# Lightning attention and a four-expert mixture on one core: unit 4's second product nested as well, attention's steps drawn together, preparation lists joined

## The chip, the core and the metric

The kernel runs on one core of a Trainium2 chip, in fp32 throughout. The metric is the device time of one execution in microseconds. The core has a matrix engine (TensorE, PE in the profile, with its weight loads as PEld), three engines for elementwise work (VectorE or DVE, ScalarE or ACT, GpSimd or POOL), and SyncE (SP), which here does nothing but issue DMA transfers. The engines run side by side, each through its own list of instructions in program order, and wait for each other by semaphores.

## The reference, cut to what matters

```python
# attention: q, k, v of (4 batches, 8 heads, 768 tokens, 64), blocks of 64 tokens, a decay lam per head
for b in range(12):
    intra = (qb @ kb^T * Dmask) @ vb                      # per batch and head
    inter = (qb * lam_pow) @ kv_state
    out[block b] = intra + inter
    kv_state = lam**64 * kv_state + (kb * rev_pow)^T @ vb
x = out of all heads side by side                         # (3072, 512)
p = domain_probs / (sum of domain_probs + 1e-9)           # (3072, 4)
for e in range(4):
    h = relu(x @ w1[e])                                   # 512 -> 1024
    y += p[:, e:e+1] * (h @ w2[e])                        # 1024 -> 512
```

The state `kv_state` goes from block to block of one batch and head, so attention has an order in time; the mixture has none, but each of its tokens needs its attention output first.

## The kernel before, in words

**Units.** The 3072 tokens are cut into three groups of 1024, each of eight chunks of 128 tokens. A unit is a group with an expert: twelve units, in the order that `ORDER` gives (group 0 with experts 0 to 3, group 1 with 1, 2, 3, 0, group 2 with 2, 3, 0, 1). A unit has a first product (x @ w1) and a second (h @ w2). Both are computed by Strassen-Winograd: seven products M1 to M7 of half-size blocks instead of eight, with sums of blocks before and after. The first product is *nested*: each of its seven products is again cut into seven, which makes 98 matmuls of 128x256 in a unit. It is `first_product`, whose matmul is line 1195. The second product exists in two forms: `second_product` (line 1254) goes one level deep, with 112 matmuls in a unit; `nested_product` (line 1571) goes two levels, with 98. `NEST` (line 140) is the first unit whose second product is nested. It is `2 * E - 3`, which is 5.

**Iterations and slots.** One iteration `at` of the main loop at the end of the kernel interweaves the second product of unit `at` with the first product of unit `at + 1`. It has seven parts `i`, one for each M, and each of those eight steps `x`. `(at * 7 + i) * 8 + x` counts the steps; I call the number a slot. The text's "unit 2" as a stretch of time is the iteration `at` = 2, slots 112 to 167.

**Attention.** Chunks 0 to 7 (group 0) are done in the prologue. Chunks 8 to 23 are spread over the iterations: `AT` (line 906) gives each its slot. At that slot the step `both` puts the values of the chunk before (`values`, matmuls at lines 842 and 860, over the state `kv` and over the masked scores) and the scores and new state of this one (`scores`, lines 779 and 786) into TensorE's order, 64x64 matmuls between the large ones. Ahead of that, counted back from the slot, come the loads (`load` of v 7 slots ahead unless `V_AHEAD` says otherwise, of k by `K_AHEAD`), the regrouping of k on ACT (`regroup`, line 526), the decay of k on POOL (`decayed`), and turning q and k on DVE (`turn`). After a pair of chunks, `pair_sums` makes sums of the x blocks on POOL (tile `to`) and stores them to `x_blocks`, from which `x_fill` loads the operands `xs` of a later group, and `x_inner` adds up more of them on POOL.

**Preparing weights.** Nested products need sums of weight blocks. They do not depend on x, and POOL makes them once for each expert, in lists of steps: load raw blocks (`w1b`, `w2b`), make totals of 512 columns (`w1o`, `w2o`), then, for each M, four sums of 256 columns (`ops`, in `inner` and `inner_w2`), and store them to DRAM (`w1_ops`, `w2_ops`, `w2_sums`). `prepare_w1`, `prepare_w2` and `prepare_w2_ops` give such lists; their steps stand in `chores`. Before, the lists follow each other whole, and that of `prepare_w2_ops(1)` is appended when `at` reaches `NEST`. The operands come back with loads named `ws_in<-w1_ops`, `w2t<-w2_sums` and `w2t<-w2_ops`.

**What sets the order.** Nothing is scheduled at run time; the Python program writes each engine's order. `pump` (line 208) is called once in every slot and takes a step from `chores` when a small model of the clock allows it: `now` counts slots, `busy` is until when POOL is estimated to be occupied (`tt`, line 116: columns / 480 slots, / 640 from unit `NEST` on, where `spare` holds), `moved` and `asked` the same for DMA. Behind a step, `pump` keeps a distance: 4 or 7 slots if `spare`, else 1. Stores are held back in `queue` by `store` until `busy` says that POOL is done. SP issues all of these loads and stores in the order of the program, each when its operands are there. `until(what)` forces steps out of `chores` until something is made, and `feed`, `feed2`, `feed3` issue the loads of products to come. DVE work that is not urgent stands in `background`, `lately`, `aside` and `own_sums`.

**The gates.** The factors p lie in `gate` (for 16 chunks) for units that are not nested. For nested units they are broadcast over the tile `decay`, which attention uses too: the load into `gate_bc` is issued at `NEST - 1`, `i` = 2, so attention has to be over by then. `turn_gates` stores the factors by rows.

**The change of form.** Group 1 begins with plain units (4 is the last of them in this kernel) and ends with nested ones. The plain unit's output rows are parked in DRAM as `partial` in the last step of unit `NEST - 1` (line 1273); in `first_result`, `gather` loads them as `po` and `finish_rows` adds them on POOL to the nested units' sums, which lie across and are turned.

Of the kernel before, what the change touches and what calls it, by code (L numbers as in the profile page):

```python
# [21 lines left out]
def kernel(  # L22
# [93 lines left out]
    def tt(eng, o, a, b, op):  # L116
        eng.tensor_tensor(out=o, in0=a, in1=b, op=op)  # L117
        if eng is nc.gpsimd:
            busy[0] = max(busy[0], now[0]) + math.prod(o.shape[1:]) / (640 if spare else 480)
        else:  # L120
            vector(math.prod(o.shape[1:]), PSUM in (a.space, b.space))
# [18 lines left out]
    NEST = 2 * E - 3  # L140
# [55 lines left out]
    LEFT, packed, resting = 1, [], [False]  # L196
    FULL = 4
# [10 lines left out]
    def pump(pace=1.0, force=False):  # L208
# [11 lines left out]
        if begins:  # L220
# [3 lines left out]
            free[0] = max(free[0], begin + max(pace * (busy[0] - was), (4 if len(chores) > 13 else 7) if spare else 1))  # L224
# [11 lines left out]
    def inner(eng, what, to, blk, ops, at):  # L236

        b = {n: blk[:, i, j * 256:(j + 1) * 256] for n, (i, j) in at.items()}
        s = stage.tile([P, 4, 256], FP32, name="ops", tag="st")
        for i, (name, x, y, op) in enumerate(ops):  # L240
            b[name] = s[:, SLOT[name]]
            tt(eng, b[name], b[x], b[y], op)
        pieces = [(to[:, 1:5], s[:])]
        if A_OF[what[2]][0] == "S":
            pieces += [(to[:, 0], blk[:, 0, 0:256]), (to[:, 5:7], blk[:, 1].rearrange("p (a f) -> p a f", a=2))]
# [12 lines left out]
    def inner_w1(e, m, blk):  # L258
        at = {"A11": (0, 0), "A21": (0, 1), "A12": (1, 0), "A22": (1, 1)}
        inner(nc.gpsimd, ("w1", e, m), w1_ops[e, MS.index(m)], blk, S_OPS, at)  # L260
# [13 lines left out]
    def prepare_w1(e):  # L274
        st = {}

        def block(name, i, j):
            t = stage.tile([P, 2, W], FP32, name="w1b", tag="st")
            src = moe_w1[e, j * 256:(j + 1) * 256, i * W:(i + 1) * W]
            send(out=t[:], in_=src.rearrange("(c p) f -> p c f", p=P))  # L280
            st[name] = t

        def total(name, a, b, op):
            t = stage.tile([P, 2, W], FP32, name="w1o", tag="st")
            halves(t[:], st[a][:], st[b][:], op)
            st[name] = t

        def ready(m):
            inner_w1(e, m, st[A_OF[m]])

        return weight_steps(block, total, ready)
# [64 lines left out]
    def prepare_w2_ops(e, eased):  # L356
# [39 lines left out]
        def drop(*names):  # L396
# [3 lines left out]
        return [  # L400
            lambda: (block("A21", 1, 0), block("A22", 1, 1)), pause(6),
            lambda: total("S1", "A21", "A22", ALU.add),
            lambda: (ready("M4"), block("A11", 0, 0), drop("A22")), pause(4),
            less, lambda: ready("M7"), lambda: (ready("M1"), drop("S3")), lambda: ready("M5"),
            lambda: (total("S2", "S1", "A11", ALU.subtract), block("A12", 0, 1)), lambda: ready("M6"),
            *([lambda: ready("M2")] if e != units[FINAL][1] else []),
            lambda: total("S4", "A12", "S2", ALU.subtract), lambda: ready("M3"),
        ]
# [21 lines left out]
    def x_fill(g, m):  # L430
# [8 lines left out]
        if g == LAST:  # L439
            own_x_apart(m, g, 8)  # L440
        else:
            chores.insert(0, lambda: x_inner(g, m))
# [175 lines left out]
    gate = consts.tile([P, LAST * CPG, E], FP32, name="gate")  # L618
# [5 lines left out]
    def gates():  # L624
# [11 lines left out]
            out=gate[:, 0:CPG].rearrange("p (h x) e -> p h x e", h=2), in_=of[:, :, 0:2].rearrange("p b c e -> p c b e"),  # L636
        )
        for g in range(1, NG):
            for h in range(2):
                n = g * CPG + h * 4  # L640
                for to in ([gate[:, n:n + 4]] if g < LAST else []) + [last[:, n - CPG:n - CPG + 4]]:
                    nc.scalar.copy(
                        out=to.rearrange("p (b c) e -> p b c e", c=2), in_=of[:, h::2, 2 * g:2 * g + 2],
                    )
# [261 lines left out]
    AT = (34, 40, 48, 54, 60, 91, 100, 108, 115, 147, 154, 167, 172, 203, 210, 223)  # L906
    K_AHEAD = {10: 14, 11: 14, 12: 15, 14: 17, 15: 18, 16: 18, 18: 17, 20: 19, 22: 17}
# [1114 lines left out]
```

## Time and profile before

| | |
|---|---|
| time, median of 3 runs | 1139.07 us (1138.53 to 1140.1) |
| profiled execution | 1138.78 us, of which the span is 1137.0 |
| PE busy | 1128.0 us (99%) |
| PEld, DVE, ACT, POOL busy | 986.1, 774.1, 445.0, 764.8 us |
| DMA | 261.36 MB, mean 230 GB/s |
| prologue, to the start of unit 0 | about 90 us |
| units 1 to 4 | 99.7, 97.6, 99.8, 94.1 us |
| units 5 and 6 | 84.6, 85.0 us |

The span runs from the first instruction to the last; about 1.8 us of the time lie around it. A unit's start is the first matmul of its iteration. In a row of the profile, L1195 is line 1195 of the kernel, then come engine, operation, tiles (out<-in) and shape; a matmul in fp32 leaves two records, so that "x8" is four matmuls of the program. L117 is the helper `tt`, through which all elementwise sums go, so those are told apart by their tiles. Row names leave the digits out: `w_ops` is `w1_ops` or `w2_ops`. In windows the columns after the length are the busy times of PE, PEld, DVE, ACT and POOL with their number of instructions, the granted clock, the DMA share and GB/s.

### The profile page before, as it was taken

What the parts mean: (1) busy time and instruction counts of PE and PEld (TensorE: products, weight loads), DVE (VectorE), ACT (ScalarE), POOL (GpSimd) and SP (SyncE); (2) the same over time, 40 slices, a digit from 0 to 9 for tenths busy, and PEclk for the clock granted to TensorE, in tenths of its full rate; (3) what the DMA queues carried; (4) which work ended last, traced back from release to release, by engine and by line L of the source; (5) the groups of instructions that cost most, each with busy time, mean ns of one, the idle gap of its engine ahead of it and who ended that gap; (6) DMA issues with size and microseconds to landing.
All of it is one profiled execution on the core that took longest, in us unless ns stands there. A gap on an engine that the chain in (4) does not pass through costs nothing.

```text
span 1137.0 us, 22208 instructions
## 1 busy us (share of the span) xinstructions
PE 1128.0 (99%) x7967; PEld 986.1 (87%) x7967; DVE 774.1 (68%) x1478; ACT 445.0 (39%) x988; POOL 764.8 (67%) x730
## 2 busy tenths in 40 slices
PE   8999999999999999999999999999999999999998
PEld 7788888888888888888888888888888888888887
DVE  4576777587587658837655566778767576776785
ACT  4325245255234534422453443344354452342332
POOL 2745547656753976644884998795984873873885
PEclk9999999999999999999999999999999999999999
DMA  9796887889896987876767669876778657656652
GB/s 200 171 281 193 227 223 233 284 273 321 259 361 209 310 270 245 286 270 216 257 195 251 189 197 319 271 225 200 224 231 253 179 161 213 188 159 205 176 195 74
DMA packets 297901, 261.36 MB, mean 230 GB/s; under 512 B 129408, under 2 KB 241216, under 8 KB 297792
## 3 DMA queue, kind: packets, MB, share of 16 engines
q1 hardware_dynamic: 287728, 255.71, 73.0%
q10 hardware_dynamic: 10032, 4.23, 1.5%
q8 instruction: 64, 1.05, 0.4%
q14 instruction: 45, 0.37, 0.1%
q0 software_dynamic: 32, 0.00, 0.0%
HBM read 192.20 MB, written 71.34 MB: 232 GB/s over the span
## 4 chain that ended last, share of the span: by engine, by line
PE 98%; DVE 1%; issue 0%; DMA 0%; ACT 0%; DVEq 0%; POOLq 0%; ACTq 0%
PE pg L1195 41%; PE pq L1571 25%; PE q L1254 21%; PE pM L1713 3%; PE pc L1713 2%; PE op L842 1%; PE sp L779 1%; PE op L860 1%; PE sp L786 1%; PE pM L1438 1%; PE pg L1571 1%; PE qp L745 0%; DMA decay<-in_lam_dram 0%; PE kp L745 0%; DVE m L117 0%
## 5 line engine op out<-in xcount | busy, mean ns | idle before, releaser
L1195 PE MATMUL pg<-xs,ws_in 128*128 128x256 f32 x1960 | 470.1, 380 | 0.1
L1195 PEld LDWEIGHTS pg<-xs,ws_in 128*128 128x128 f32 x1960 | 371.1, 190 | 52.5 <-DVE m L117 2.1
L117 DVE TENSOR_TENSOR m<-pg,m 128x512 f32<-128x512 f32 x374 | 255.3, 685 | 96.9 <-PE pg L1195 87.5
L1254 PE MATMUL q<-w2t,m 128*128 128x256 f32 x1120 | 265.4, 380 | 0.0
L1254 PEld LDWEIGHTS q<-w2t,m 128*128 128x128 f32 x1120 | 212.1, 190 | 29.6 <-issue 0.6
L117 DVE TENSOR_TENSOR sums<-pq,sums 128x256 f32<-128x256 f32 x272 | 112.9, 420 | 90.6 <-PE pq L1571 75.2
L117 POOL TENSOR_TENSOR m<-m,decay 128x512 f32<-128x512 f32 x91 | 114.5, 1271 | 85.9 <-ACT m L1212 64.6
L1571 PE MATMUL pq<-acc,w2t 128*128 128x256 f32 x688 | 169.2, 379 | 0.0
L1571 PEld LDWEIGHTS pq<-acc,w2t 128*128 128x128 f32 x688 | 130.6, 190 | 17.9
L1212 ACT ACTIVATE m<-m 128x512 f32<-128x512 f32 x99 | 62.3, 630 | 154.4 <-DVE m L117 152.3
L117 DVE TENSOR_TENSOR m<-m,m 128x512 f32<-128x512 f32 x108 | 96.9, 898 | 7.8 <-ACT m L1178 7.0
L1208 ACT COPY m<-pg 128x512 f32<-128x512 f32 x88 | 51.5, 586 | 123.4 <-PE pg L1195 115.8
L1272 DVE SCALAR_TENSOR_TENSOR acc<-q,gate,acc 128x256 f32<-128x256 f32 x108 | 52.0, 481 | 69.9 <-PE q L1254 68.9
L1172 ACT COPY pg<-m 128x512 f32<-128x512 f32 x77 | 45.4, 590 | 103.0 <-DVE m L117 88.2
L117 POOL TENSOR_TENSOR acc<-hT,hT 128x512 f32<-128x512 f32 x56 | 70.4, 1271 | 22.6 <-PE pq L1571 13.2
L117 POOL TENSOR_TENSOR acc<-hT,acc 128x512 f32<-128x512 f32 x56 | 71.2, 1272 | 6.5 <-PE pq L1571 2.9
L526 ACT COPY kx<-kn 32x128 f32<-32x128 f32 x224 | 66.2, 295 | 12.8 <-PE op L860 5.1
L1571 PE MATMUL pq<-hT,w2t 128*128 128x256 f32 x288 | 70.0, 379 | 0.0
L117 POOL TENSOR_TENSOR w2o<-w2b 128x512 f32<-128x512 f32 x26 | 35.6, 1391 | 49.2 <-DMA w2b<-in_moe_w_dram 38.2
L1571 PEld LDWEIGHTS pq<-hT,w2t 128*128 128x128 f32 x288 | 54.7, 190 | 7.4
L1176 ACT COPY m<-pg 128x512 f32<-128x512 f32 x44 | 25.7, 585 | 77.0 <-PE pg L1195 70.7
L1571 PE MATMUL pq<-m,w2t 128*128 128x256 f32 x228 | 55.4, 379 | 0.0
(158 smaller groups left out, 1465.2 us busy)
## 6 DMA issues: line engine op xcount, KB each, us to landing
ws_in<-w_ops SPq DMA_DIRECT2D x40, 512.0 KB, 4.8
w2t<-w_ops SPq DMA_DIRECT2D x72, 256.0 KB, 3.1
ws_in<-w_ops SPq DMA_DIRECT2D x60, 256.0 KB, 3.6
ws_in<-w_ops SPq DMA_DIRECT2D x40, 384.0 KB, 3.8
w2b<-in_moe_w_dram SPq DMA_DIRECT2D x56, 256.0 KB, 5.5
w_ops<-ops SPq DMA_DIRECT2D x28, 512.0 KB, 4.7
w_ops<-ops SPq DMA_DIRECT2D x54, 256.0 KB, 3.8
w2t<-w_ops SPq DMA_DIRECT2D x100, 128.0 KB, 2.7
```

The costliest lines, as they stand in the source:

```text
L117: eng.tensor_tensor(out=o, in0=a, in1=b, op=op)
L526: nc.scalar.copy(out=to[j * 32:(j + 1) * 32, :, x], in_=of[x * 32:(x + 1) * 32, :, j // 2, j % 2 * 32:(j % 2 + 1) * 32],)
L779: nc.tensor.matmul(out=sp[r][half[x], ac * BL:(ac + 1) * BL], lhsT=hc(kT)[half[r], ac, blk[x]], rhs=hc(qT)[half[r], ac, blk[x]], start=(ac ...
L1172: nc.scalar.copy(out=banks[tags[1]][:], in_=new["11"][:])
L1176: nc.scalar.copy(out=o[:], in_=p[:])
L1195: nc.tensor.matmul(out=p[:, j * 256:(j + 1) * 256], lhsT=ws[i][:, j * P:(j + 1) * P], rhs=xs[i], start=(fresh and j == 0), stop=True, skip ...
L1208: nc.scalar.copy(out=new[at][:], in_=p[:])
L1212: nc.scalar.activation(out=new[at][:], in_=new[at][:], func=AF.Relu)
L1254: nc.tensor.matmul(out=p[:, s * DH:(s + 1) * DH], lhsT=h[A_OF[m]][:, c * 256 + s * P:c * 256 + (s + 1) * P], rhs=fed2[g, e, m][uu][:, c], ...
L1272: nc.vector.scalar_tensor_tensor(out=o, in0=x, scalar=w, in1=o, op0=ALU.mult, op1=ALU.add)
L1571: nc.tensor.matmul(out=p[:, 0:256], lhsT=fed3[e, m, i][:, c * P:(c + 1) * P], rhs=b[B_OF[i]][:, c * 256:(c + 1) * 256], start=(fresh and c ...
L1713: nc.tensor.matmul(out=p[:, s * 256:(s + 1) * 256], lhsT=a[c][:, f:f + P], rhs=b[:, c, j * 256:(j + 1) * 256], start=(s == 0 and c == 0 an ...
```

## The change

- `NEST` becomes `2 * E - 4`: unit 4, the first of group 1, has its second product nested too. Group 1 is now nested as a whole, so `partial`, its stores, loads and additions go, and `gate` keeps group 0 alone.
- Attention's slots are drawn together: the last chunk's scores are at slot 172 (iteration 3) instead of 223. Chunks named in `ALONE` (12, 13, 17, 18 and the last) get a slot of their own for their values, so these no longer stand beside the next chunk's scores; scores at certain slots go to the PSUM banks s0 and s1. `V_AHEAD` goes, `K_AHEAD` is shorter.
- The lists of preparation are joined by `in_turn`: the first step of a list, its raw loads, is put ahead of the last two steps of the list before. `prepare_w2_ops(1)` is now the fourth list, from the start. M2's sums are made in all eased lists.
- The model's POOL cost becomes 0.13 + n/770 slots (0.2 + n/820 with `spare`) for n columns, and `pump` keeps 3 slots with `spare` behind a step that used POOL, else 1.
- `prepare_w1` and `inner` get an `eased` form, which is not called; the condition on `SEQ.index(m)` in `x_fill` always holds.

```diff
-    NEST = 2 * E - 3
+    NEST = 2 * E - 4
...
-            busy[0] = max(busy[0], now[0]) + math.prod(o.shape[1:]) / (640 if spare else 480)
+            n = math.prod(o.shape[1:])
+            busy[0] = max(busy[0], now[0]) + (0.2 + n / 820 if spare else 0.13 + n / 770)
...
-            free[0] = max(free[0], begin + max(pace * (busy[0] - was), (4 if len(chores) > 13 else 7) if spare else 1))
+            free[0] = max(free[0], begin + max(pace * (busy[0] - was), 3 if spare and busy[0] > was else 1))
...
+    def in_turn(*lists):
+
+        work = []
+        for of in lists:
+            n = OVER if work else 0
+            work[len(work) - n:] = [of[0], *work[len(work) - n:], *([] if n else of[1:2]), *of[2:]]
+        return work
...
-            *([lambda: ready("M2")] if e != units[FINAL][1] else []),
...
-    gate = consts.tile([P, LAST * CPG, E], FP32, name="gate")
+    gate = consts.tile([P, CPG, E], FP32, name="gate")
...
-    AT = (34, 40, 48, 54, 60, 91, 100, 108, 115, 147, 154, 167, 172, 203, 210, 223)
-    K_AHEAD = {10: 14, 11: 14, 12: 15, 14: 17, 15: 18, 16: 18, 18: 17, 20: 19, 22: 17}
-    V_AHEAD = {CPG + 10: 8, CPG + 13: 10}
+    AT = (34, 40, 48, 54, 60, 72, 91, 100, 108, 115, 130, 146, 153, 160, 167, 172)
+    ALONE = {CPG + 4: 66, CPG + 5: 79, CPG + 9: 124, CPG + 10: 137, NG * CPG - 1: 178}
+    LEAD = {}
+    K_AHEAD = {10: 14, 11: 14, 12: 15}
...
-            def both(n=n):
-                if n > first:
+            def both(n=n, s=s):
+                if n > first and n - 1 not in ALONE:
                     values(n - 1, ("s0", "s1"))
-                scores(n, ("q02", "q12"))
+                scores(n, ("s0", "s1") if 8 <= s % 56 < 32 else ("q02", "q12"))
...
-            steps.append((s - V_AHEAD.get(n, 7), lambda n=n: load(n, "v")))
+            steps.append((s - 7, lambda n=n: load(n, "v")))
...
+            if n in ALONE:
+                steps.append((ALONE[n], lambda n=n: values(n, ("s0", "s1"))))
-        steps.append((AT[last - first] + 5, lambda: values(last, ("s0", "s1"))))
-        steps.append((AT[last - first] - 14, turn_gates))
+        steps.append((ALONE[last] + 2, turn_gates))
...
-        while unit_of[g, e] in (1, 2 * E) and to_do.get(m):
+        while unit_of[g, e] in (1, E, 2 * E) and to_do.get(m):
...
-            if unit_of[g, e] in (E - 1, NEST - 1) and m in ("M2", "M6", "M5", "M3"):
-                to = rows[n] if g == 0 else partial[n % CPG * P:(n % CPG + 1) * P]
-                results.append(lambda: send(out=to[:, j * DH:(j + 1) * DH], in_=o))
+            if unit_of[g, e] == E - 1 and m in ("M2", "M6", "M5", "M3"):
+                results.append(lambda: send(out=rows[n][:, j * DH:(j + 1) * DH], in_=o))
...
-            tt(nc.gpsimd, t[:], t[:], po[:], ALU.add)
-            store(lambda: send(out=rows[CPG + n], in_=t[:]))
+            t = gathered_out.pop(n)
+            send(out=rows[CPG + n], in_=t[:])
...
-            chores.extend(prepare_w2(2) + prepare_w1(3) + prepare_w2(3))
-            chores.extend(prepare_w2_ops(2, False) + prepare_w1(0))
-            for x in (3, 0):
-                chores.extend(prepare_w2_ops(x, True))
+            chores.extend(in_turn(
+                prepare_w2(2), prepare_w1(3), prepare_w2(3), prepare_w2_ops(1, False), prepare_w2_ops(2, False),
+                prepare_w1(0), prepare_w2_ops(3, True), prepare_w2_ops(0, True),
+            ))
...
-            until(("w1", 0, "M4"))
-            chores.extend(prepare_w2_ops(1, True))
+            until(("w2", 1, "M4"))
             spare.append(True)
```

## The prediction

> **What bounds the kernel.** I read the page's busy shares first, then the chain that ended last, the windows cut at the units, and last TensorE's records around one chunk of attention.
>
> ```profile
> span 1137.0 us, 22208 instructions
> PE 1128.0 (99%) x7967; PEld 986.1 (87%) x7967; DVE 774.1 (68%) x1478; ACT 445.0 (39%) x988; POOL 764.8 (67%) x730
> PE 98%; DVE 1%; issue 0%; DMA 0%; ACT 0%; DVEq 0%; POOLq 0%; ACTq 0%
> ```
>
> TensorE is busy for 99% of the span and carries 98% of the chain, so the time is the matmuls that the program holds plus the few waits that it gets. Taking work off another engine is worth nothing here. The windows are those of units 1 to 6 and, last, 20 us inside unit 2:
>
> ```profile
> 187.80:287.50 99.70, 99.70 (x933) 87.19 (x932) 73.27 (x142) 42.36 (x115) 63.94 (x69) 1.00 0.87 284
> 287.50:385.10 97.60, 97.60 (x789) 85.11 (x788) 69.57 (x127) 41.69 (x111) 60.60 (x65) 1.00 0.91 294
> 385.10:484.90 99.80, 99.80 (x902) 87.22 (x901) 68.78 (x126) 37.81 (x101) 71.26 (x82) 1.00 0.85 269
> 484.90:579.00 94.10, 94.10 (x598) 82.83 (x598) 56.37 (x97) 29.80 (x58) 56.59 (x61) 1.00 0.74 244
> 579.00:663.60 84.60, 84.60 (x393) 74.34 (x392) 47.27 (x83) 38.70 (x80) 68.11 (x63) 1.00 0.65 205
> 663.60:748.60 85.00, 84.94 (x393) 74.31 (x393) 62.39 (x124) 32.39 (x59) 74.40 (x71) 1.00 0.84 270
> 325.00:345.00 20.00, 20.00 (x94) 17.34 (x93) 18.16 (x26) 10.18 (x29) 12.28 (x9) 1.00 1.06 377
> ```
>
> After the length come the busy times of PE, PEld, DVE, ACT and POOL, the clock, the DMA share and GB/s. TensorE never idles in units 1 to 5; a nested unit without attention (5) takes 84.6 us. Where unit 2 is densest, DVE is busy 18.2 us of 20 and DMA moves 377 GB/s, and TensorE still does not wait.
>
> ```profile
> 446.60 1.89 PE L1195 MATMUL pg<-xs,ws_in 128*128 128x256 f32 x8
> 448.42 0.69 PE L842 MATMUL op<-qx,kv 64*64 64x64 f32 x32
> 448.94 0.65 PE L860 MATMUL op<-st,vn 64*64 64x64 f32 x32
> 449.40 0.65 PE L779 MATMUL sp<-qx,kx 64*64 64x64 f32 x32
> 449.87 0.65 PE L786 MATMUL sp<-vn,kn 64*64 64x64 f32 x32
> 450.44 1.99 PE L1254 MATMUL q<-w2t,m 128*128 128x256 f32 x8
> 452.28 0.59 PE L1195 MATMUL pg<-xs,ws_in 128*128 128x256 f32 x2
> ```
>
> One chunk's values and the next one's scores stand together: a stretch of 64x64 matmuls between the large ones.
>
> **The change, part by part.** *Matmuls.* Counted in the two programs, L1254 goes from 560 to 448 large matmuls and L1571 from 602 to 700: 112 out, 98 in. Eight records (four matmuls of 128x256) follow each other in 1.727 us, 0.432 us for one. 14 fewer: -14 x 0.432 = **-6.05 us**, all on the path. It is also the difference between a plain unit (210 x 0.432 = 90.7) and the 84.6 of unit 5.
>
> *More stretches.* The 64x64 matmuls stay the same in number, but chunks with a step of their own split their stretch: counted from chunk 8 on, 17 stretches become 21. From 446.60 to 452.28 are 5.68 us: two large batches of 1.727 (3.45), four small ones of 0.466 (1.87), and 0.36 us for going in and out. 4 x 0.36 = **+1.44 us**. The stretch around 496 us (two small batches) leaves the same 0.36.
>
> *Work that moves.* Attention's last chunk goes from slot 223 to 167-178, so units 1 and 2 take six chunks or so where they had four. By their matmuls unit 1 becomes 90.7 + 20 x 0.466 + 7 x 0.36 = 102.6 us, unit 2 with 19 small batches 102.1.
>
> POOL in unit 2, counted by kind and multiplied by the page's rows: the 256-column list operations on `ops` go from 28 to 48 (21.6 to 36.0 us), the 512-column totals on `w2o` and `w1o` from 14 to 18 (19.3 to 24.5), and two more chunks bring two `kn` at 1.1, two `kv` at 0.78 and four `to` at 0.81 (7.1). In all 64.7 to 91.3 us of 102.1. Unit 1 goes from 66.6 to 74.6, unit 3 from 66.4 to 81.6, unit 4 from 55.8 to 75.8, unit 5 from 70.0 to 81.1 of 84.7. Units 3 to 5 I cost at nothing: unit 6 now does 74.4 us on POOL in 85.0 with TensorE busy 84.94, and a list that is late in unit 5 can run on in unit 6, which falls from 78.3 to 60.9.
>
> SP in unit 2: the `w2_ops` stores go from 6 to 36, those of `w1_ops` from 8 to 0, the `w2b` loads from 14 to 10, those of a chunk (`kn`, `qx`, `vn`) from 12 to 17; +3.8 MB. In unit 1 the `w2b` loads go from 8 to 22, stores and chunk loads grow by 7; +5.5 MB. SP issues in order, so every store stands with the loads behind it until POOL has done its operands: in unit 1 to 2 that was 12.3 us over 8 waits, longest 5.9. Unit 1 needs 28.3 + 5.5 = 33.8 MB in 102.6 us, 330 GB/s; unit 2 28.7 + 3.8 = 32.5 MB, 318 GB/s. At their present GB/s for a share (284/0.87, 294/0.91) that is a share of 1.01 and 0.99.
>
> [...]
>
> What this can cost, from both sides. Nothing, if all stays covered as between 325 and 345 us; less than nothing only by TensorE's own waits, 5.6 us in all, of which I grant 1.1. At the upper end POOL's chain in unit 2 is the bound:
>
> ```profile
> POOL xs L117 <- DMA xs<-x_blocks: 12.7, 1, 12.7
> POOL w2o L117 <- DMA w2b<-in_moe_w_dram: 10.9, 2, 8.4
> POOL kn L117 <- ACT kx L526: 7.4, 1, 7.4
> POOL to L117 <- DVE xc L117: 3.2, 1, 3.2
> ```
>
> These are POOL's waits in unit 2. The `w2b` one should go, since each list's first raw loads are now issued two steps before the last list ends. If the other 23.3 us stay, 91.3 + 23.3 = 114.6 us must fit in 102.1: 12.5 us late. Set beside the start of the matmul that reads it, the k decay on POOL now ends at least 6.0 us early, so TensorE would stand 6.5 us, or all 12.5 if that slack is used up as well. I take **+1.5 us**: the 20 us with everything full and no wait are the nearest row, and above it I allow a wait as long as the longest that a chunk now has on ACT's `kv` (1.0), and half of another.
>
> *At nothing.* Gone are 16 `partial` stores, 8 loads and 8 POOL additions of 1.272 us: all in nested units whose TensorE does not idle; they also take 3.1 MB off DMA there. DVE gains 49 `sums` at 0.420 and loses 24 `m<-m,m` at 0.898 and 28 `acc` at 0.481; unit 2's DVE rises from 76.3 to 83.6 of 102.1, below the 91% that the 20 us show covered. ACT's 46 to 60 us there are far from a bound. The planner's POOL cost (n/480 to 0.13 + n/770) and the pump's spacing only move the list steps that are counted above.
>
> *Sum.* The profiled execution took 1138.78 us (span 1137.0 and 1.8 around it), 0.29 below the median. 1138.78 - 6.05 + 1.44 + 1.5 = 1135.67; with the 0.29, **1136.0 us**.
>
> **The rivals.** *Loads late (the gain is eaten).* Set beside its first matmul, the tightest `ws_in` load of `w1_ops` now lands 2.9 us ahead, in unit 1. If one store in each of units 1 and 2 holds SP for the 5.9 us seen there, the loads behind it are 3.0 us late each: 6 us instead of 1.5, so 1134.5 + 6 = 1140.5; with one of them 1137.5. For it: DMA shares near 1.0, and six times as many stores of `w2_ops` behind POOL. Against it: the median slack of these loads is 13.5 us, and raw loads move ahead. I take 1139.
>
> *POOL becomes the bound of unit 2 (the other side).* The longer chain of list operations in front of the chunks' decays makes TensorE stand in the last chunks of unit 2, where three of them follow at every seventh slot (146, 153, 160). 6.5 to 12.5 us give 1141.0 to 1147.0; middle 1144. It decides from 4.6 us of waits on: there the gain is gone; from 6.9 on the loss can be measured. For it: 91.3 of 102.1 us, in an engine that takes its work in program order. Against it: the planner spaces the list steps, and the wait for `xs` is in part room that POOL had to spare, as its work ran ahead.
>
> *The change does not nest unit 4.* The order has the 98 matmuls, so this has no chance.
>
> **How the numbers follow.** The forecast has a chance of 0.45, late loads 0.20, POOL's bound 0.35. 0.2% (2.3 us) is about what a measurement can tell from no change: faster is below 1136.8, slower above 1141.35. So faster 0.45, same 0.20, slower 0.35. The range runs from 1134.5 - 1.1 = 1133.4 to the end of the third case, 1147.0; the forecast alone holds 1133.4 to 1136.8.
>
> **What the profile after would show.** The chain still at 98% PE; unit 4 near 85.0 us and units 1 and 2 at 102.6 and 102.1 if nothing waits; 21 stretches. Any excess in units 1 to 3 is the error: by POOL's bound it stands as idle of L779/L786 or L842 behind POOL `kn` or `qx` in unit 2, with POOL above 90%; by late loads as idle of L1195 behind `ws_in`. I am wrong on the other parts if units 5 to 11 change by more than 0.3 us each, or if a stretch costs other than 0.36.

## The result, and the profile after

The changed kernel takes 1165.45 us (median of 6 runs, 1161.67 to 1167.11) against 1139.64 us before: a ratio of 1.0222, 95% interval 1.0207 to 1.0237. It is 2.2% slower; I had forecast 1136.0 us. Its profiled execution, at 1161.67 us, is the fastest of the six. What follows compares its span of 1159.5 us with the 1137.0 us of before.

The page of the changed kernel: span, busy times, the chain by engine.

```profile
span 1159.5 us, 22257 instructions
PE 1130.7 (98%) x7939; PEld 982.2 (85%) x7939; DVE 786.0 (68%) x1502; ACT 453.4 (39%) x1003; POOL 817.3 (70%) x767
PE 65%; POOL 2%; DMA 2%; DVE 1%; ACT 0%; issue 0%; SPq 0%; POOLq 0%; DVEq 0%; ACTq 0%
```

TensorE has 28 records (14 matmuls) fewer and is busy for longer; its part of the chain falls from 98% to 65%. The shares add up to 70%, since the chain could be followed back only to about 332 us; even on that part POOL, DMA and DVE hold 5 of 70. Something other than TensorE sets the time in places. To see where, I cut both traces at the first first-product matmul of iterations 1, 2, 3 and 4. First before, then after; columns as earlier (length, then busy PE, PEld, DVE, ACT, POOL, clock, DMA share, GB/s).

```profile
189.50:289.30 99.80, 99.80 (x934) 87.25 (x933) 73.06 (x141) 42.35 (x115) 64.78 (x68) 1.00 0.86 282
289.30:389.00 99.70, 99.70 (x902) 87.14 (x901) 70.25 (x124) 42.46 (x115) 62.62 (x68) 1.00 0.92 298
389.00:488.70 99.70, 99.70 (x902) 87.17 (x901) 68.25 (x124) 37.78 (x100) 71.08 (x81) 1.00 0.85 266
```

```profile
189.60:305.60 116.00, 104.00 (x1061) 88.86 (x1059) 83.27 (x157) 47.14 (x133) 87.33 (x89) 0.99 0.89 297
305.60:421.10 115.50, 109.44 (x1140) 94.05 (x1141) 72.38 (x139) 53.31 (x155) 83.41 (x91) 0.96 0.91 284
421.10:517.50 96.40, 95.13 (x598) 82.41 (x598) 61.61 (x105) 29.91 (x59) 86.99 (x96) 1.00 0.85 283
```

Units 1 and 2 are longer by 16.4 and 15.8 us (99.7 to 116.1 and to 115.5), unit 3 is shorter by 3.4, unit 4 by 7.2 (91.9 to 84.7). Unit 0 is longer by 0.9 and unit 6 by 1.0; all other units agree within 0.1 us. POOL is busy for only 75% and 72% of units 1 and 2, DMA stands at 0.89 and 0.91: neither is full, and TensorE waits all the same. These are TensorE's waits in the changed kernel between 187 and 420 us (what waited and for whom; total, times, longest), below them those of POOL between 187 and 450 us from 1.4 us up, and last POOL's waits for stores in the kernel before, in the same stretch.

```profile
PE pg L1234 <- DMA ws_in<-in_moe_w_dram: 8.1, 2, 5.8
PE sp L823 <- POOL kn L117: 6.4, 2, 5.5
PE pg L1234 <- DVE m L117: 1.8, 2, 1.0
PE sp L823 <- issue: 1.8, 2, 1.3
```

```profile
POOL w2o L117 <- DMA x_blocks<-to: 17.7, 1, 17.7
POOL ops L117 <- DMA w_ops<-ops: 9.3, 1, 9.3
POOL w2o L117 <- DMA w2b<-in_moe_w_dram: 8.0, 2, 5.1
POOL xs L117 <- DMA xs<-x_blocks: 7.7, 2, 4.6
POOL w2o L117 <- DMA w_ops<-ops: 7.6, 1, 7.6
POOL w2o L117 <- DMA w_sums<-w2o: 5.5, 1, 5.5
POOL kn L117 <- ACT kx L563: 1.5, 1, 1.5
POOL to L117 <- DMA w_sums<-w2o: 1.4, 1, 1.4
```

```profile
POOL w1o L117 <- DMA x_blocks<-to: 2.5, 1, 2.5
POOL ops L117 <- DMA w_ops<-ops: 1.0, 1, 1.0
POOL w2o L117 <- DMA w_ops<-ops: 0.5, 1, 0.5
```

The rows that matter name a *store* as what POOL waits for: `x_blocks<-to`, `w_ops<-ops`, `w_sums<-w2o`. `w2o` and `ops` are not computed from those transfers. They are tiles of the same staging ring (`stage`, seven buffers for raw blocks, totals, sums and `to`), and a new tile may be written only when the one that had its buffer has been stored. 17.7 + 9.3 + 7.6 + 5.5 + 1.4 = 41.5 us go this way. In the kernel before it was 4.0 us.

How this reaches TensorE is seen in the order of time up to 310 us: POOL, then SP, then TensorE.

```profile
287.90 2.51 POOL L117 TENSOR_TENSOR w2o<-w2b 128x512 f32<-128x512 f32 x2 [7.61 <-DMA w_ops<-ops]
292.86 2.50 POOL L117 TENSOR_TENSOR w2o<-w2b 128x512 f32<-128x512 f32 x2
...
319.45 5.57 POOL L117 TENSOR_TENSOR w2o<-w2b,w2o 128x512 f32<-128x512 f32 x4 [17.72 <-DMA x_blocks<-to]
```

```profile
273.44 1.93 SPq L114 DMA_DIRECT2D w2b<-in_moe_w_dram  x4
275.47 2.01 SPq L114 DMA_DIRECT2D w2t<-in_moe_w_dram  x2
277.53 0.46 SPq L114 DMA_DIRECT2D ws_in<-in_moe_w_dram  x1
...
290.96 0.74 SPq L114 DMA_DIRECT2D w_sums<-w2o  x1
295.39 2.93 SPq L114 DMA_DIRECT2D w2b<-in_moe_w_dram  x6
298.41 0.89 SPq L114 DMA_DIRECT2D w2t<-w_sums  x2
299.35 0.46 SPq L114 DMA_DIRECT2D ws_in<-in_moe_w_dram  x1
```

```profile
283.42 1.97 PE L1234 MATMUL pg<-xs,ws_in 128*128 128x256 f32 x8 [2.38 <-DMA ws_in<-in_moe_w_dram]
...
298.00 1.89 PE L1293 MATMUL q<-w2t,m 128*128 128x256 f32 x8
305.64 3.68 PE L1234 MATMUL pg<-xs,ws_in 128*128 128x256 f32 x8 [5.75 <-DMA ws_in<-in_moe_w_dram]
309.16 1.89 PE L1293 MATMUL q<-w2t,m 128*128 128x256 f32 x8
```

POOL stood 7.6 us for a buffer and made the `w2o` total at 292.9 to 295.4. From 291.7 on SP stood 3.6 us in front of six raw loads (`w2b`) of the next list, until the end of that total on POOL released them: a raw load, too, needs a buffer of the ring. It then came to the `ws_in` load at 299.35; TensorE could have used it at 299.9 and got it at 305.6. The `ws_in` load of 277.53, for which TensorE waited 2.4 us, stood in the same way behind raw loads, in front of which SP had waited 6.2 us for POOL's `w1o`. So what held SP ahead of both late loads were raw loads issued early, and not stores. In units 1 and 2 SP stood 14.1 us at raw loads in this way.

The next eight large records after the wait took 3.68 us instead of 1.89: the granted clock was 0.59 in the window from 305 to 310 us. The second long wait, 5.5 us at 370 us, is a k decay that stands behind `ops` sums which POOL could begin only after 9.3 us of waiting for a buffer. The store that ended those 9.3 us was issued at 364.9 us, behind a third hold of SP at raw loads, 4.3 us until 358.2. SP's order has a part in the longest wait of POOL as well: `to` was made at 301.7 us, its store was issued only at 311.0 and landed at 319.3. The ring and SP's order thus hold each other.

### The profile page after: what moved, and what is told of

Read it like the earlier page. It is cut to its first block, busy times and chain, and to the rows that moved or that the text cites. A ratio compares the mean times of both kernels' runs of the same rounds, so it can differ in the third digit from the quotient of the medians.

```text
span 1159.5 us, 22257 instructions
## 1 busy us (share of the span) xinstructions
PE 1130.7 (98%) x7939; PEld 982.2 (85%) x7939; DVE 786.0 (68%) x1502; ACT 453.4 (39%) x1003; POOL 817.3 (70%) x767
## 4 chain that ended last, share of the span: by engine, by line
PE 65%; POOL 2%; DMA 2%; DVE 1%; ACT 0%; issue 0%; SPq 0%; POOLq 0%; DVEq 0%; ACTq 0%
PE pg L1234 30%; PE pq L1606 28%; PE q L1293 5%; DMA w_ops<-ops 1%; POOL ops L117 1%; DVE m L117 1%; POOL w2o L117 1%; PE pM L1475 1%; PE pg L1606 1%; DMA w2b<-in_moe_w_dram 0%; PE op L879 0%; PE sp L823 0%; PE op L897 0%; PE yp L1435 0%; PE sp L816 0%
## 5 line engine op out<-in xcount | busy, mean ns | idle before, releaser
L1293 PE MATMUL q<-w2t,m 128*128 128x256 f32 x896 | 212.4, 380 | 0.0
L117 POOL TENSOR_TENSOR m<-m,decay 128x512 f32<-128x512 f32 x104 | 130.9, 1274 | 111.9 <-ACT m L1251 72.7
L117 DVE TENSOR_TENSOR sums<-pq,sums 128x256 f32<-128x256 f32 x321 | 133.5, 421 | 106.3 <-PE pq L1606 91.9
L1606 PE MATMUL pq<-acc,w2t 128*128 128x256 f32 x800 | 196.8, 379 | 0.0
L1293 PEld LDWEIGHTS q<-w2t,m 128*128 128x128 f32 x896 | 170.0, 190 | 23.7 <-issue 0.3
L1606 PEld LDWEIGHTS pq<-acc,w2t 128*128 128x128 f32 x800 | 151.9, 190 | 20.8
L1247 ACT COPY m<-pg 128x512 f32<-128x512 f32 x88 | 51.5, 585 | 109.1 <-PE pg L1234 106.7
L1211 ACT COPY pg<-m 128x512 f32<-128x512 f32 x77 | 45.2, 588 | 119.1 <-DVE m L117 108.9
L117 DVE TENSOR_TENSOR m<-m,m 128x512 f32<-128x512 f32 x84 | 78.5, 936 | 2.7 <-ACT m L1217 2.4
L1065 ACT COPY hp<-m 128x512 f32<-128x512 f32 x96 | 55.4, 589 | 18.2 <-DVE hT L117 15.2
L117 POOL TENSOR_TENSOR acc<-m,acc 128x512 f32<-128x512 f32 x44 | 56.0, 1272 | 3.4
```

What stands on the lines that cost most here:

```text
L1065: nc.scalar.copy(out=there[x][:], in_=blk[at][:])
L1211: nc.scalar.copy(out=banks[tags[1]][:], in_=new["11"][:])
L1247: nc.scalar.copy(out=new[at][:], in_=p[:])
L1293: nc.tensor.matmul(out=p[:, s * DH:(s + 1) * DH], lhsT=h[A_OF[m]][:, c * 256 + s * P:c * 256 + (s + 1) * P], rhs=fed2[g, e, m][uu][:, c], ...
L1606: nc.tensor.matmul(out=p[:, 0:256], lhsT=fed3[e, m, i][:, c * P:(c + 1) * P], rhs=b[B_OF[i]][:, c * 256:(c + 1) * 256], start=(fresh and c ...
```

## The experiments

All changes are made to the changed kernel where nothing else is said. Each run's time is one execution, beside one of before on the same chip (1137.86 for the first four, 1138.52, 1137.84 and 1140.74 for the next three lots), except for the last two runs, which were timed in rounds. Repeats of one kernel lie 5.4 us apart (the changed kernel) and 7.4 us (the last run but one), so a few microseconds between single runs say little; the lengths of the units, read from the traces, say more.

### Which part: loads ahead, attention, POOL's work, or the timing of stores

```diff
-    OVER = 2
+    OVER = 1
```

> The changed kernel with the raw loads of a list put ahead of the last step of the list before, instead of its last two (OVER = 1). Buffers theory: the loads ahead hold the ring of seven staging buffers, so POOL has to wait until its own stores have landed (41.5 us of such waits in units 1 to 3 of the changed kernel, the longest 17.7), and the stores stand in SP's order behind what waits for POOL. Loads one step later hold them for less time: those waits fall under 20 us, the time to 1140 to 1155 us. POOL-work theory: POOL has the same instructions to do, 91 us in unit 2, and the time stays within 4 us of 1165.

Measured: 1146.1 us; 19 of the 26 us are gone. POOL's waits in units 1 to 3 were these (rows on other releasers are left out):

```profile
POOL w2o L117 <- DMA w2b<-in_moe_w_dram: 9.6, 3, 4.0
...
POOL w2o L117 <- DMA w_sums<-w2o: 7.5, 2, 4.8
POOL ops L117 <- DMA x_blocks<-to: 4.0, 1, 4.0
...
POOL w2o L117 <- DMA w_ops<-ops: 2.6, 1, 2.6
```

Waiting for stores fell from 41.5 to 14.1 us, with the same instructions on POOL (817.3 us busy in both). SP's stand at raw loads in units 1 and 2 fell from 14.1 to 0.2 us, and TensorE's waits for `ws_in` from 8.1 to 2.5. In unit 1 POOL was even busier than in the changed kernel (93.1 us against 87.3, and 81.6 against 83.4 in unit 2). That is as the buffers theory had it, and it speaks against POOL's work as the cause.

The kernel before, with the changed kernel's `AT`, `ALONE`, `K_AHEAD` and `attention`:

```diff
-    AT = (34, 40, 48, 54, 60, 91, 100, 108, 115, 147, 154, 167, 172, 203, 210, 223)
+    AT = (34, 40, 48, 54, 60, 72, 91, 100, 108, 115, 130, 146, 153, 160, 167, 172)
+    ALONE = {CPG + 4: 66, CPG + 5: 79, CPG + 9: 124, CPG + 10: 137, NG * CPG - 1: 178}
```

> The kernel before with the changed kernel's slots of attention alone (AT, ALONE, K_AHEAD, no V_AHEAD); unit 4 stays plain, the lists and the planner as before. Attention theory: the denser chunks in units 1 and 2, with their loads, are what makes TensorE wait: 1150 us or more, with waits of L823's line on POOL kn and of the first product on ws_in. Buffers theory and POOL-work theory: four more stretches at 0.36 us, 1141 us, up to 1144 with a wait or two.

Measured: 1141.63 us, with no wait of TensorE listed between 187 and 450 us. Units 1 to 4 took 103.5, 105.5, 94.3 and 90.6 us, 2.8 us more than before. Attention's denser slots are cheap by themselves, as the second theory had it.

The list of expert 1's w2 sums left out, expert 2's read in its place:

```diff
-                prepare_w2(2), prepare_w1(3), prepare_w2(3), prepare_w2_ops(1, False), prepare_w2_ops(2, False),
+                prepare_w2(2), prepare_w1(3), prepare_w2(3), prepare_w2_ops(2, False),
...
-            until(("w2", x_e, m))
+            until(("w2", x_e if x_e != 1 else 2, m))
...
-            until(("w2", 1, "M4"))
+            until(("w2", 2, "M4"))
```

> The changed kernel without the list that prepares expert 1's weight sums for the nested second product; units that need them read expert 2's instead, so the output of expert 1 in groups 1 and 2 is not the reference's. POOL has some 36 us less to do in units 1 to 3. POOL-work theory: TensorE no longer waits in units 1 and 2, 1134 to 1138 us. Buffers theory: the other lists are still interwoven and hold the staging buffers, so a third to a half of the waits stay: 1142 to 1152 us.

Measured: 1156.74 us, slower than either theory gave. POOL had 30.5 us less to do in the whole run (786.8 against 817.3 busy), but in units 1 and 2 it was busy as before, 86.3 and 83.6 us against 87.3 and 83.4: the lists behind the missing one moved up into its place. So the run does not test POOL's work there. It shows that the waits for stores (16.9, 8.6, 6.7 and 5.6 us) do not hang on that one list.

```diff
-        queue.append((busy[0] + (8 if spare else 2), f))
+        queue.append((busy[0] + (8 if spare else 4), f))
```

> The changed kernel with each store held back for 4 slots behind the modelled end of POOL's work instead of 2. SP-order theory: SP stands at stores whose operands POOL has not made (about 60 us of waits of SP on POOL in units 1 to 3), and the loads of ws_in behind them come late; later stores take half of that away, and the time falls to 1145 to 1155 us. Buffers theory: the buffers come free later still, POOL waits longer for its stores, and the time stays at 1160 or rises over 1170.

Measured: 1169.16 us. Later stores do not help; the longest wait for a buffer stays at 17.5 us. But SP's waits for POOL between 187 and 420 us stayed too, at 66.3 us against 67.2, so the edit did not relieve SP and cannot decide about SP's order. `pump` issues all held stores but one whenever it begins a list step, whatever their delay, which may be why.

### Where the lists stand

```diff
-                prepare_w2(2), prepare_w1(3), prepare_w2(3), prepare_w2_ops(1, False), prepare_w2_ops(2, False),
-                prepare_w1(0), prepare_w2_ops(3, True), prepare_w2_ops(0, True),
+                prepare_w2(2), prepare_w1(3), prepare_w2(3), prepare_w2_ops(2, False), prepare_w1(0),
+                prepare_w2_ops(1, False), prepare_w2_ops(3, True), prepare_w2_ops(0, True),
```

with `OVER = 1`:

> The changed kernel with raw loads one step ahead (OVER = 1) and expert 1's list of w2 sums moved from the fourth place to the sixth, behind prepare_w1(0). Buffers theory: with one step ahead 1146.1 us were left; the order of the lists changes little in the number of buffers that are held, so 1138 to 1146. POOL-work theory: the 36 us of the list move into units 3 and 4 and out of units 1 and 2, so the waits of units 1 and 2 go wholly: 1135 to 1138 us.

Measured: 1140.81 us. Units 1 to 4 took 106.8, 106.6, 95.3 and 84.7 us; TensorE's waits in them came to some 5 us, none above 1.6. In the fourth place the first three took 108.3, 106.8 and 95.3 us: the place is worth 1.7 us. Most of the other 3.6 us lie ahead of unit 0, whose first product began at 86.6 us here and at 89.7 there. POOL's busy time in units 1 and 2 did not fall (92.5 and 83.0 us), since other lists moved up, so POOL's work is not tested by this run either.

The same order with `OVER = 0`:

> As the run before it in this list, but with the lists one behind the other and not interwoven at all (OVER = 0), so that a list's raw loads are issued only behind the last step of the list before. Buffers theory: POOL waits no longer for its own stores to land (under 5 us in units 1 to 3), TensorE's waits in units 1 and 2 are gone, 1134 to 1138 us; POOL waits for raw loads instead, as in the kernel before. If raw loads ahead were a help, this is slower than the run with one step ahead.

Measured: 1166.4 us, which I had not expected at all. For units 1 and 2 the forecast was nearly right: POOL's waits for stores were 3.0 us in all, TensorE's waits some 3 us, and the two units took 210.8 us together, against 231.6 in the changed kernel. But unit 4 took 107.9 us. TensorE's and POOL's lines there:

```profile
516.66 3.78 PE L1606 MATMUL pq<-acc,w2t 128*128 128x256 f32 x8 [16.16 <-ACT sums L1614]
```

```profile
510.77 1.40 POOL L117 TENSOR_TENSOR ops<-w2b 128x256 f32<-128x256 f32 x2
512.25 0.72 POOL L117 TENSOR_TENSOR ops<-ops,w2b 128x256 f32<-128x256 f32 x1
513.05 0.72 POOL L117 TENSOR_TENSOR ops<-w2b,ops 128x256 f32<-128x256 f32 x1
513.73 2.48 POOL L117 TENSOR_TENSOR w2o<-w2b,w2o 128x512 f32<-128x512 f32 x2
```

From 497 to 516 us POOL works through what is left of the lists, one sum behind the other, at the start of unit 4, where `until(("w2", 1, "M4"))` forces it out ahead of the unit's own work. Expert 1's sums have a due time now, which they did not have when unit 4 was plain. With the list in the sixth place, loads ahead are what meets it. Two things are not told apart here: `in_turn` also drops the pause of 4 or 6 slots behind the raw loads of a joined list, and whole lists keep it. And whole lists with expert 1's in the fourth place were not run; they might be done in time.

Expert 1's list fifth, with `OVER = 1`:

> The changed kernel with raw loads one step ahead and expert 1's list in the fifth place, behind expert 2's. Both theories: between the 1146.1 us of the fourth place and what the sixth place gives; the buffers theory expects the difference between places to stay under 5 us.

Measured: 1144.34 us, between the fourth place (1146.1) and the sixth (1140.81), but that order is mostly chance: units 1 to 3 took 308.8 us, against 310.4 and 308.7, and the first product began at 89.5 us, against 89.7 and 86.6.

### What a wait costs by itself

```diff
+            for _ in range({(7, 3): 30, (8, 3): 45, (9, 3): 60, (10, 2): 80}.get((at, i), 0)):
+                nc.gpsimd.tensor_tensor(out=tiny[:], in0=tiny[:], in1=tiny[:], op=ALU.add)
```

> The kernel before with 30, 45, 60 and 80 idle additions of 16 columns on POOL put in front of its work in iterations 7, 8, 9 (part 3) and 10 (part 2), where no attention and no list runs: it measures what a late operand costs TensorE by itself, wait and clock apart. By the changed kernel's trace a wait of 5.5 us or more is followed by eight large records at half the rate, 1.9 us more, and one of 2.8 us by none. If that holds, waits of under 2.8 us lengthen the time by themselves alone and those above 5.5 us by 1.9 us more. If the clock goes by something else than the length of one wait, a short wait can bring the slow records too, as one of 1.8 us seems to have done in the run with stores held longer.

Measured: 1147.77 us. The additions took 0.215 us each. The 30, 45 and 80 were covered and did not lengthen their units; the 60 gave one wait:

```profile
969.46 1.03 PE L1573 MATMUL pq<-hT,w2t 128*128 128x256 f32 x4
974.43 1.13 PE L1573 MATMUL pq<-acc,w2t 128*128 128x256 f32 x4 [3.95 <-POOL acc L117]
975.40 3.35 PE L1197 MATMUL pg<-xs,ws_in 128*128 128x256 f32 x8
```

The unit grew from 84.7 to 90.6 us: 4.1 us of waiting and 1.8 more of slow records. A wait of 3.95 us was enough for the slow records. The length of one wait does not decide below that: 3.45 us were followed by full speed (the run of 1145.95 us with three lists ahead, below), 2.15 us by eight records in 3.54 us (ACT issuing in the changed kernel, below), and in the run with stores at 4 slots even 1.6 us by eight in 3.64 us. The 45 additions, 9.7 us, were covered in full, so at that place POOL had that much room.

### The middle ground: cost, pieces, stores

All four start from the kernel of 1140.81 us (OVER = 1, expert 1's list sixth). The old POOL cost:

```diff
-            n = math.prod(o.shape[1:])
-            busy[0] = max(busy[0], now[0]) + (0.2 + n / 820 if spare else 0.13 + n / 770)
+            busy[0] = max(busy[0], now[0]) + math.prod(o.shape[1:]) / (640 if spare else 480)
```

> The kernel of 1140.8 us (raw loads one step ahead, expert 1's list sixth) with the planner's old POOL cost (n/480, n/640 with spare): for 512 columns 1.07 slots instead of 0.79, so steps stand further apart and stores are held longer. If the new, tighter cost is part of the loss: fewer of the 41 us in which SP waits for POOL in units 1 to 3, and 1137 to 1140 us. If the lists only need to be done in time: they become late for unit 4, as with the whole lists (a wait of 16 us there), 1145 to 1165 us.

Measured: 1184.72 us, above both ranges; the lists were late for unit 4, as in the second. SP waited only 15.0 us on POOL's `ops`, and unit 1 took 103.2 us; units 3 and 4 took 116.4 and 103.0, with waits of 18.7 and 13.4 us around unit 4's start. The due time is missed here though the lists are joined.

```diff
-            n = OVER if work else 0
+            n = 0 if not work else 1 if of is lists[5] else 0
```

> As the kernel of 1140.8 us, but only expert 1's list has its raw loads one step ahead; all other lists stand whole behind each other. Buffers theory: units 1 and 2 as with whole lists (210.8 us for the two instead of 213.4), and unit 4's wait of 16.5 us at its start remains in good part, since the lists ahead of expert 1's are as late as there: 1148 to 1164 us.

Measured: 1163.5 us. Unit 1 took 104.6 us, unit 4 108.4 with a wait of 15.6 at its start.

```diff
+            n = 0 if not work else 1 if of in lists[3:6] else 0
```

> As the kernel of 1140.8 us, but only the fourth to sixth list (w2 sums of expert 2, w1 of expert 0, w2 sums of expert 1) have their raw loads one step ahead; the first three stand whole. Buffers theory: the waits of unit 1 (3.7 us in gaps) come from the first three lists, which end there, and fall to 2 us or less, while the later lists still end in time: 1137 to 1141 us. If the time gained by the early loads in unit 1 is needed at unit 4, a wait at its start comes back: 1143 to 1155 us.

Measured: 1145.95 us, the second branch. Units 1 and 2 took 104.9 and 105.4 us, and waits of 3.5 and 2.0 us came back around unit 4's start: units 3 and 4 took 98.4 and 86.9 us. 2.4 of the 5.1 us between the two runs lie ahead of unit 0.

```diff
+        queue.append((busy[0] + (8 if spare else 1), f))
```

> As the kernel of 1140.8 us, with each store held back for 1 slot behind the modelled end of POOL's work instead of 2. Buffers theory: the buffers come free sooner, 1139 to 1141 us. SP-order theory: SP stands longer at stores that POOL has not made and the loads behind them are later: 1142 to 1150 us.

Measured: 1150.51 us, just above the second range; SP's waits for POOL's `ops` rose from 35.3 to 45.2 us, unit 1 from 106.8 to 112.7 us. But in unit 1 alone SP's waits for `ops` were 20.9 us against 19.9. TensorE's longest wait there, 3.1 us at 226.4 us, ended when a load of v landed that SP had issued at 218.0. That SP's order made it late is likely and not shown; POOL's waits for stores rose as well, from 11.0 to 16.3 us.

### Taking the stores out of SP's order

The lists' three `send` calls in `store` get `by=nc.gpsimd` or `by=nc.scalar`. In the changed kernel, POOL issuing:

> The changed kernel with the lists' stores (w1_ops, w2_ops, w2_sums) issued by POOL itself instead of SP; all else as it is, raw loads two steps ahead. SP no longer stands at a store that POOL has not made, so the loads of ws_in behind it go out in time and the buffers come free without waiting for SP's order. SP-order theory (SP's order is the link through which POOL and the loads hold each other): the 41.5 us in which POOL waits for its stores and buffers fall under 15, TensorE's waits in units 1 and 2 under 5 us, 1138 to 1148 us, plus what POOL spends on issuing, which no trace here shows. Buffers theory without SP: seven buffers are too few for loads that far ahead, whoever issues the stores; 1155 us or more.

Measured: 1224.52 us, far above the first range and inside the open second one. POOL has 151 more instructions and is busy 891.2 us instead of 817.3, 0.49 us for each:

```profile
L114 POOL DMA_DIRECT2D w_ops<-ops x77 | 43.2, 562 | 0.0
```

TensorE then waited 26.8 us for `kn`. POOL still waited 47.1 us for stores to land, and TensorE 10.6 us for `ws_in`, though the lists' stores no longer stood in SP's order. So these waits do not need SP standing at the lists' stores; but POOL's own issuing weighs on all of this, and the time says little of the theories.

ACT issuing:

```diff
-        store(lambda: ([send(out=x, in_=y) for x, y in pieces], made.add(what)))
+        store(lambda: ([send(out=x, in_=y, by=nc.scalar) for x, y in pieces], made.add(what)))
```

> The same with ACT issuing the lists' stores. ACT stands at them in SP's place, where it copies first-product sums and regroups k. SP-order theory: SP's waits on POOL (60 us in units 1 to 3) go, but ACT's take their place; 1145 to 1165 us, with TensorE waiting on ACT's pg or on kx instead of ws_in. Buffers theory: 1160 us or more.

Measured: 1164.59 us, which both theories allow, so the waits have to tell. The longest of TensorE between 187 and 480 us, then POOL's for stores:

```profile
PE pg L1234 <- ACT pg L1211: 13.9, 5, 6.4
PE pg L1234 <- ACT m L1247: 2.1, 2, 1.1
```

```profile
POOL w2o L117 <- DMA x_blocks<-to: 11.0, 1, 11.0
POOL ops L117 <- DMA w_ops<-ops: 10.1, 1, 10.1
...
POOL w2o L117 <- DMA w_sums<-w2o: 5.1, 1, 5.1
POOL w2o L117 <- DMA w_ops<-w1o: 5.1, 1, 5.1
```

TensorE waits no longer for `ws_in`, but for ACT's copies. ACT stands at the stores now: its regrouping of k (`kx`) waited 8.4 us for POOL's `ops`, which it does not read. SP still stands at raw loads in front of the `ws_in` loads, 9.3 us at 272.0 and 2.8 at 290.9, so its order is not freed; TensorE is late for another reason first. And POOL still waits 31.3 us for buffers: whoever issues the stores, that is left.

The same two moves in the kernel of 1140.81 us:

> The kernel of 1140.8 us (one step ahead, expert 1's list sixth) with ACT issuing the lists' stores. SP still waits 41 us for POOL there. SP-order theory: the 5 us of TensorE's waits in units 1 and 2 go, 1135 to 1138 us, unless ACT's standing costs more; then 1141 to 1150.

> The kernel of 1140.8 us with POOL issuing the lists' stores itself. SP-order theory: TensorE's waits in units 1 and 2 go, 1135 to 1138 us, if POOL's time for issuing about 110 stores is small; if each costs POOL about as much as an operation of 256 columns (0.76 us), POOL is short of time in units 2 and 3 and expert 1's list is late at unit 4: 1145 to 1160 us.

Measured: 1145.95 us with ACT, the second case (unit 1 112.7 us; 4.8 us of TensorE's waits are on ACT), and 1237.56 us with POOL, where I had priced an issue at up to 0.76 us and still came out 77 us too low at best. In this kernel the lists' stores cost least on SP.

### The last two settings

From the kernel of 1140.81 us, the old spacing from unit 4 on, and stores held for 3 slots:

```diff
-            free[0] = max(free[0], begin + max(pace * (busy[0] - was), 3 if spare and busy[0] > was else 1))
+            free[0] = max(free[0], begin + max(pace * (busy[0] - was), (4 if len(chores) > 13 else 7) if spare else 1))
```

> The kernel of 1140.8 us (one step ahead, expert 1's list sixth) with the old spacing of the list steps from unit 4 on (4 or 7 slots instead of 3 behind a step that used POOL). Units 1 to 3 are ordered as there. If the new spacing belongs to the loss, the 1.1 us by which unit 6 is longer than before go: 1139.7 us. If the lists of experts 3 and 0 then end late, a wait comes at unit 6 or 7: 1142 us or more.

Measured: 1144.6 us, ratio 1.0057 (1.0037 to 1.0076). Unit 6 stays at 86.1 us, so the spacing is not its cause. All units agree with the kernel of 1140.81 us to 0.1 us; the profiled spans differ by 2.1 us because the first product begins 2.0 us later (88.6 against 86.6 us). That one run of 1140.81 us was a lucky one in its prologue. The time lies in the second range, but chance put it there: no wait came at unit 6 or 7.

> The kernel of 1140.8 us with stores held back for 3 slots instead of 2; 1 slot gave 1150.5. SP-order theory: SP waits less for POOL (35 us there in units 1 to 4), the loads behind go out in time: 1138 to 1140.5 us. Buffers theory: the staging buffers come free later and POOL waits longer for them: 1142 to 1147 us.

Measured: 1142.6 us, ratio 1.0021 (1.0010 to 1.0032). That is in the range of the buffers theory, which I had set beside the lucky run; POOL's waits for stores did not grow (9.6 us against 11.0), and units 1 to 3 took 308.5 us against 308.7. Of the versions with unit 4 nested that were timed in rounds, this is the fastest, and it is still 0.2% slower than the kernel before. None of the versions was faster than the kernel before on its chip.

## Why the prediction was wrong, by its steps

- **Matmuls, -6.05 us: right.** With attention's slots alone, unit 4 took 90.6 us; nested, 84.7. That is 5.9.
- **Stretches, +1.44 us: right, but not all of it.** The run with attention alone paid 2.8 us in units 1 to 4. A stretch costs 0.36 us there too: from 206.73 to 211.47 us are 4.74, less two large batches (3.45) and two small ones (0.93). Four make 1.4 us; the other 1.3 lie in delays of under 0.3 us each that no view lists.
- **Waits, +1.5 us: this is the step that failed.** Units 1 to 3 took 328.0 us in the changed kernel and 303.3 with attention alone: 24.7 us, twice even the upper end of 12.5. Of these, 18.1 are TensorE's waits that the views list, and 3.7 the two phases of slow records behind them. Half of the loss is in unit 1, for which the forecast priced no wait and put POOL's work at 74.6 us, where it was 87.3 (12.6 us are lost there, 10.0 in unit 2, 2.1 in unit 3). The upper end was worked out from four rows of POOL's waits, one of which I struck out with "The `w2b` one should go, since each list's first raw loads are now issued two steps before". It did fall, from 23.7 us in units 1 to 3 to 8.0. What I left out is what the early loads occupy: the ring of seven buffers. Of waits for a buffer the trace before showed 4.0 us, and I priced their growth at nothing; they became 41.5. The early raw loads, for which no buffer was free, stood in SP's order as well, 14.1 us in units 1 and 2.
- **"Nothing, if all stays covered as between 325 and 345 us": the wrong row.** In that window DVE was busy for 18.16 us of 20 and DMA's share was 1.06, at 377 GB/s, and TensorE did not wait. The window says nothing of a POOL that stands.
- **POOL becomes the bound of unit 2: right side, right symptom, wrong mechanism.** TensorE did wait 5.5 us for a `kn` at 370 us, but POOL was busy for 72% of the unit, not above 90%. With one step ahead POOL had as much to do in units 1 and 2, and TensorE's waits above 2.5 us went. My sum of work and remaining waits could not show this, since the waits for buffers went by the order: with the same 817.3 us of work on POOL they were 41.5 us two steps ahead and 14.1 one step ahead.
- **Loads late: it was the link in unit 1, through another instruction.** Two `ws_in` loads cost 8.1 us there. I had expected SP to stand at stores, up to 5.9 us, and had counted "raw loads move ahead" against this rival. It was the raw loads at which SP stood, 6.2 and 3.6 us. Its longest hold at a store, 9.6 us up to 322.4, delayed no load that TensorE waited for.
- **"At nothing", the planner's cost: wrong.** I had it only move list steps. In the kernel with one step ahead the old cost made 1184.72 us of 1140.81.
- **DMA's share** was put at 1.01 and 0.99. It is 0.89 and 0.91 in the longer units of the changed kernel, and 0.98 and 0.99 at 326 and 311 GB/s in the kernel of 1140.81 us, whose TensorE waits some 5 us. Bandwidth was not what made the difference.
- **The clock was not in the sum.** Two phases of slow records cost 1.8 and 1.9 us.
- **Units 5 to 11** were to stay within 0.3 us: they did but for unit 6, which is 1.0 us longer, and at least as much in every version with unit 4 nested. Its cause is open; the spacing is ruled out.

What the runs show as a whole: nesting unit 4 gives expert 1's sums a due time. With the list sixth it is met by early loads and a tight cost; with whole lists or the old cost TensorE waits 13 to 19 us around unit 4's start. Two steps ahead, the lists hold the ring: POOL waits for its own stores, SP stands at raw loads for which no buffer is free, and TensorE gets operands late. One step ahead loses least on both ends, wherever the list stands. In the sixth place units 1 to 3 still take 5.4 us more than with attention alone, which is about what the 14 matmuls give. That the ring's size as such is the limit was argued from the tiles and the effect of `OVER`; a kernel with more buffers was not run.

## What to carry to other kernels

In these traces POOL's sums waited up to 17.7 us for stores whose data they do not read: what they waited for was a buffer of the ring. Where a trace shows such a wait, count how many tiles of the ring are alive at once before issuing loads earlier. Ask as well what stands in front of such a load in the queue that issues it, and what stands behind: here raw loads without a buffer, at which SP stood 6.2 and 3.6 us, kept back loads that TensorE needed. An edit that moves preparation forward has two ends, a due time and the buffers it holds, and a price for it has to be worked out at both. In the run with POOL held, a wait of 3.95 us on the matrix engine was followed by slow records that cost 1.8 us more.

## What the runs showed of the hardware that was not expected

- After some waits, TensorE ran about eight large records at about half the rate: 3.35 to 3.78 us instead of 1.89, with a granted clock of 0.59 in the window from 305 to 310 us of the changed kernel. Waits of 3.95, 5.53, 5.75 and 16.16 us were followed by such records. Of the shorter ones, 1.61 and 2.15 us were too, 2.38 and 3.45 us were not. What decides in short waits, the runs do not show.
- Issuing a transfer on POOL took 0.49 us of POOL's time (73.9 us more busy for 151 more instructions), and 0.56 us as the mean of 77 of them in the profile.
- A load that waits for its buffer kept back the transfers behind it in SP's order: SP stood 6.2 and 3.6 us at such loads, and two loads behind them came 2.4 and 5.8 us late for TensorE.
